# Attention and conv-gated feed-forward: from a hand-written opening and half-tile steps to periods of a whole tile

## The chip, the cores and the metric
One NeuronCore of a Trainium2 chip. TensorE (PE) multiplies matrices, with weight loads of its own (PEld); VectorE (DVE), ScalarE (ACT) and GpSimd (POOL) work elementwise; SyncE (SP) issues transfers. The metric is device microseconds of one execution. The kernel before took 697.51 us in the median of 3 runs (697.41 to 699.11).

## The reference
Eight batches of 576 tokens with 8 heads of 64: attention with a causal window of 128 tokens and a linear bias, then a feed-forward block with a gate from a convolution over three neighbouring tokens.

```python
scores = q @ k.T / 8 + slope[h] * -abs(i - j)     # where 0 <= i - j < 128, else -1e9
x = softmax(scores) @ v                           # heads side by side: (8, 576, 512)
h = maximum(x @ w_in, 0)                          # 512 -> 1024
conv = sum(conv_w[k] * h[token + k - 1] for k in range(3))
out = (h * sigmoid(conv)) @ w_out                 # 1024 -> 512
```
q, k and v are 32-bit floats; the three weight arrays are 64-bit floats, which the kernel turns into 32-bit ones on the core.

## The kernel before
The 4608 tokens are 36 tiles of 128. A tile goes through the attention in two halves (`u` = 0, 1) of four heads each:
- `load`, `loadv` (L198, L204): SP transfers q and k into `rqk`, v into `rv`.
- `qkT` (L212): PE transposes q and k (`pt`), ACT copies them to `qkT_all`.
- `scores` (L221): PE writes scores of this and the previous tile of keys to two PSUM tiles `sc` per half; DVE puts the mask in (L246) and adds the bias with a row minimum (L261), ACT exponentiates (L271), DVE divides by the sum (L279 to L281). The result is `e`.
- `attnT` (L284): PE transposes `e` (`pa`), ACT copies it to `rl` (L291), POOL cuts it into the part of this tile and of the previous one (L294, L297).
- `av` (L302), for both halves at once: PE multiplies with v, ACT and DVE split the result into a high and a low part in `x` (L323, L324). `xfin` (L335) copies one column to the neighbouring chunk (L338, L340).

The feed-forward block works on chunks of two tiles, in four steps a chunk. `up` (L349): two blocks of 12 matmuls `p` (L360), then ReLU, the convolution and the gate on ACT and DVE (`hh`, `z`), split into `gh` and `gl`. `down` (L389): 12 matmuls into `o` (L401), two steps behind `up`; after the fourth the result is copied and transferred out.

The weights come in 16 blocks of 128 x 512 and one of convolution weights. Each is transferred into `wst` (512 KB; two buffers), ACT and DVE turn its words into f32 in `wg` (`to_f32`, L122: one ACT operation, four of DVE, L129 to L136), and ACT and POOL split it into a high and a low part (L149, L150). The first two blocks go by ACT's queue into the buffer `wearly` (L163), 1 MB in all, at the very start.

All `sc`, `pt`, `pa`, `av` and `p` tiles take their PSUM banks in turn from one pool of six; `o` has two others.

The order of PE's work is the order in which the program issues it (`manual_schedule`, L487). A list of tokens, `START` (L419), writes the opening out by hand: each token is one step (`q` qkT, `c` scores, `t` attnT, `a` av, `f` a feed-forward step, `w` a weight block, `l`, `r` loads), its number a half tile (a tile, for loads). Then `STEADY` (L426) repeats once for each half tile: scores, loads, a transpose two halves ahead, attnT one half behind, av two halves behind, a feed-forward step. The other engines' orders are set by a planner from the same program and from priorities (`PRIORITY`, L427); every engine then works through its list in that order, waiting for semaphores.

Of the kernel before, what the change touches and what calls it, by code (L numbers as in the profile page):

```python
# [16 lines left out]
P = 128  # L17
# [4 lines left out]
def tile_alibi_window_attention_conv_glu(  # L22
# [31 lines left out]
    def as32(ap):  # L54
        return ap.bitcast(F32)
# [61 lines left out]
    def words(src):  # L117
        return src.bitcast(U32).rearrange("p (n t) -> p n t", t=2)
# [22 lines left out]
    def fetch_weight(src, st, eng):  # L141
        eng.dma_start(out=st, in_=words(src))
        return st

    def load_weight(dst, src, col, st=None):
        if st is None:
            st = fetch_weight(src, wpool.tile([P, WB, 2], U32, name="wst", tag="wst"), nc.sync)
        f = to_f32(st, wpool.tile([P, WB], I32, name="wg", tag="wg"))
        nc.scalar.copy(out=dst[0][:, col, :], in_=f)  # L149
        nc.gpsimd.tensor_tensor(out=dst[1][:, col, :], in0=f, in1=as32(dst[0][:, col, :]), op=ALU.subtract)  # L150

    def load_conv():
        n = 3 * NFC
        st = wpool.tile([P, WB, 2], U32, name="wst", tag="wst")[:n, :P, :]
        nc.sync.dma_start(out=st, in_=moe_conv_w.rearrange("k (f p) -> (k f) p", p=P).bitcast(U32).rearrange("r (p t) -> r p t", t=2))
        f = to_f32(st, wpool.tile([P, WB], I32, name="wg", tag="wg")[:n, :P])
        ps = pst.tile([P, n], F32, name="pcw", tag="tr")
        nc.tensor.transpose(ps, f, ident[:n, :n])
        nc.vector.tensor_copy(out=cw.rearrange("p k f -> p (k f)"), in_=ps)

    early = {}

    def fetch_early(c):  # L163
        if c == 0:
            early["t"] = xpool.tile([P, 2, WB, 2], U32, name="wearly", tag="x")
        early[c] = early["t"][:, c]
        fetch_weight(moe_w_in[c * P : (c + 1) * P, :WB], early[c], nc.scalar)

    def weight_items():
        for part in range(DFF // WB):  # L170
            for c in range(NCC):
                src = moe_w_in[c * P : (c + 1) * P, part * WB : (part + 1) * WB]
                yield lambda c=c, part=part, src=src: load_weight(
                    [w[:, :, part * WB : (part + 1) * WB] for w in wi], src, c, early[c] if part == 0 and c < 2 else None
                )
        yield load_conv
        for f in range(NFC):
            yield lambda f=f: load_weight(wo, moe_w_out[f * P : (f + 1) * P, :], f)

# [235 lines left out]

    START = """  # L419
    e0 e1 l0 r0 q1 w l1 q0 c0 w r1 q2 l2 w r2 c1 l3 t0 q3 t1 a0 c2 q4 w c3 w r3 t2 a1 q5 c4   # L420
    t3 a2 w q6 q7 c5 l4 t4 a3 w r4 c6 w w t5 a4 w l5 w w q8 r5 w c8 c7 w t6
    a5 q9 f w q10 c9 l6 a6 l7 t7 r6 w q12 w t8 f a7 q11 c10 t9 a8 f f a9 c12 
    t10 q13 q14 c11 a10 f l8 r7 r8 t11 c13 q15 t12 f a11
    """
# [4 lines left out]
    NU = 2 * NT  # L429
    NFP = NFC // 2  # L430
    downs, fns, done = [], {}, set()

    wpool = ctx.enter_context(tc.tile_pool(name="wpool", bufs=2))
    weights = list(weight_items())
    todo = [(c, i) for c in range(NCH) for i in range(NFP)]
    pos = 0

    def ffn_step(c, i):
        if c not in fns:
            fns[c] = ffn_items(c)  # L440
        fns[c][0](i)
        downs.append((c, i))
        if len(downs) > 2:
            cc, ii = downs.pop(0)
            fns[cc][1](ii)

    def step(kind, n):
        nonlocal pos
        if kind == "w":
            if weights:  # L450
                weights.pop(0)()
            return
        if kind == "f":
            if pos < len(todo):
                ffn_step(*todo[pos])
                pos += 1
            return
        if (kind, n) in done or n < 0 or n >= (NT if kind in "lr" else NU):
            return
        done.add((kind, n))  # L460
        t, u = divmod(n, 2)
        if kind == "e":
            fetch_early(n)
        elif kind == "l":
            load(n)
        elif kind == "r":
            loadv(n)
        elif kind == "q":
            qkT(t, u)
        elif kind == "c":  # L470
            scores(t, u)
        elif kind == "t":
            attnT(t, u)
        elif kind == "a":
            if u == 1:
                av(t)
                xfin(t)

    def run(kind, n=-1):
        if kind in PRIORITY:  # L480
            with tc.high_priority(PRIORITY[kind]):
                step(kind, n)
        else:
            step(kind, n)


    with tc.manual_schedule(engines={mybir.EngineType.PE}):  # L487
        for token in START.split():
            run(token[0], int(token[1:] or -1))
        n = 0  # L490
        while pos < len(todo) or n < NU + 3:
            for _ in range(3 if n else 2):
                run("w")
            t, u = divmod(n, 2)
            for token in STEADY.split():
                kind, d = token[0], int(token[1:] or 0)
                if kind in "lr":
                    if u == 1:
                        run(kind, t + d)
                elif kind == "f":  # L500
                    if n >= LAG + pos + (pos >= NFP):
                        run("f")
                else:
                    run(kind, n + d)
            n += 1
        for cc, ii in downs:
            fns[cc][1](ii)


# [26 lines left out]
```

## Time and profile before

| | us |
|---|---|
| median of 3 runs | 697.51 |
| profiled execution | 698.46 |
| its span, first to last instruction | 696.7 |
| PE busy in the span | 645.9 |
| DVE busy | 488.8 |
| ACT busy | 452.7 |
| POOL busy | 205.5 |

The span falls into an opening of about 98.6 us, in which PE has gaps, a middle up to the last `av` at about 645.4 us, and a tail of feed-forward steps. Busy times are sums over an engine's instructions; PE's matmuls overlap in the pipeline, so how long a block of matmuls holds PE is read from its start to the next block's start, not from its printed length. A granted clock of 1.00 is 2.4 GHz; the other level is half of it, 1.2 GHz, and a stretch between them has had both.

### The profile page before, as it was taken

The numbers are of one execution on the slowest core, as the hardware profiler recorded it, in microseconds if no ns is written. First come the engines' busy times: TensorE is split into PE (matmuls) and PEld (weight loads), VectorE is DVE, ScalarE is ACT, GpSimd is POOL, SyncE is SP. The second block draws the span as 40 slices with busy tenths as digits, with TensorE's granted clock in tenths as the row PEclk, the third lists the DMA queues.
The fourth block names the chain that finished last, engine by engine and source line by source line (L and its number), as shares of the span: only waits on it lengthen the run. The fifth ranks groups of instructions, "written<-read, shape, count | busy, mean of one in ns | idle before, by whom it ended". The sixth has DMA issues, their size and how long they took to land.

```text
span 696.7 us, 13447 instructions
## 1 busy us (share of the span) xinstructions
PE 645.9 (93%) x4833; PEld 546.6 (78%) x4833; DVE 488.8 (70%) x1584; ACT 452.7 (65%) x1258; POOL 205.5 (29%) x233
## 2 busy tenths in 40 slices
PE   3664489999999999999999999999999999999997
PEld 2443378888888888888888888888888888888996
DVE  6888987667776777677676677667776777677442
ACT  3664576767676767676767676767676667665563
POOL 2353442322222222222222222222222222222221
PEclk9978699999999999999999999999999999999999
DMA  9454522222322222222312222222222222000000
GB/s 247 116 152 137 137 47 47 77 47 77 62 61 47 77 46 77 47 76 47 92 31 76 47 77 46 77 47 76 62 62 46 77 47 77 16 31 1 31 32 30
DMA packets 120102, 47.02 MB, mean 67 GB/s; under 512 B 113356, under 2 KB 113380, under 8 KB 120036
## 3 DMA queue, kind: packets, MB, share of 16 engines
q1 hardware_dynamic: 119748, 45.12, 25.8%
q10 hardware_dynamic: 288, 1.05, 0.4%
q8 instruction: 38, 0.62, 0.4%
q14 instruction: 28, 0.23, 0.1%
HBM read 36.72 MB, written 9.44 MB: 66 GB/s over the span
## 4 chain that ended last, share of the span: by engine, by line
PE 86%; DVE 9%; DMA 2%; ACT 2%; issue 1%; SPq 0%; ACTq 0%
PE p L360 30%; PE o L401 28%; PE sc L239 9%; PE av L315 8%; PE pt L218 5%; PE pa L288 4%; DVE wg L136 1%; DVE sc L246 1%; DVE wst L135 1%; DVE sc L261 1%; DMA wst<-in_moe_w_out_dram 1%; DMA rqk<-in_k_dram 1%; DVE e L281 1%; DVE z L373 1%; ACT e L271 1%
## 5 line engine op out<-in xcount | busy, mean ns | idle before, releaser
L360 PE MATMUL p<-x,wi 128*128 128x258 f32 x1728 | 229.5, 290 | 7.8 <-ACT wg L128 7.8
L360 PEld LDWEIGHTS p<-x,wi 128*128 128x128 f32 x1728 | 216.5, 193 | 14.2 <-ACT wg L128 8.1
L386 POOL TENSOR_TENSOR gl<-z,gh 128x512 fp32r<-128x512 f32 x72 | 92.3, 1281 | 372.9 <-ACT gh L385 368.5
L401 PE MATMUL o<-wo,gh 128*128 128x512 f32 x576 | 180.8, 395 | 0.0
L373 DVE SCALAR_TENSOR_TENSOR z<-hh,cw,z 128x256 f32<-128x256 f32 (+7 forms) x384 | 145.9, 424 | 35.2 <-ACT z L366 32.2
L401 PEld LDWEIGHTS o<-wo,gh 128*128 128x128 f32 x576 | 103.5, 188 | 19.7
L271 ACT ACTIVATE e<-sc,st 128x128 f32<-128x128 f32 x288 | 106.3, 376 | 15.9 <-DVE st L261 11.7
L401 PE MATMUL o<-wo,gl 128*128 128x512 f32 x288 | 113.9, 396 | 0.0
L261 DVE CUSTOM_DVE_ANT_0 sc<-sc,bias 128x128 f32<-128x128 f32 x288 | 81.6, 303 | 44.0 <-ACT e L271 44.0
L379 ACT ACTIVATE z<-z 128x512 f32<-128x512 f32 x72 | 45.5, 632 | 77.4 <-DVE z L373 77.2
L365 ACT ACTIVATE hh<-p 128x258 f32<-128x258 f32 x144 | 56.1, 390 | 45.0 <-PE p L360 44.6
L380 DVE SCALAR_TENSOR_TENSOR z<-z,hh 128x512 f32<-128x512 f32 x72 | 49.8, 691 | 48.0 <-ACT z L379 48.0
L239 PE MATMUL sc<-qkT_all 64*128 64x256 f32 x512 | 76.5, 420 | 6.2 <-ACT qkT_all L219 6.2
L366 ACT ACTIVATE z<-hh,cw 128x256 f32<-128x256 f32 x144 | 74.3, 516 | 5.7
L239 PEld LDWEIGHTS sc<-qkT_all 64*128 64x128 f32 x512 | 46.6, 196 | 31.2 <-issue 14.3
L315 PE MATMUL av<-rl,rv 128*64 128x128 f32 x1088 | 69.8, 282 | 0.0
L385 ACT CAST gh<-z 128x512 fp32r<-128x512 f32 x72 | 44.6, 620 | 37.5 <-DVE z L380 37.4
L315 PEld LDWEIGHTS av<-rl,rv 128*64 128x64 f32 x1088 | 60.9, 141 | 6.8 <-issue 6.6
L401 PEld LDWEIGHTS o<-wo,gl 128*128 128x128 f32 x288 | 54.1, 188 | 13.0
L288 PE MATMUL pa<-ident_r,e 128*128 128x128 f32 x288 | 45.9, 284 | 19.3 <-DVE e L281 16.5
L218 PE MATMUL pt<-ident_r,rqk 128*128 128x128 f32 x288 | 49.9, 301 | 12.4 <-DMA rqk<-in_q_dram 6.2
L246 DVE COPY_PREDICATED sc<-m_prev,sc 128x256 f32<-128x256 uint8 x128 | 49.5, 425 | 16.0 <-PE sc L239 15.7
(62 smaller groups left out, 623.2 us busy)
## 6 DMA issues: line engine op xcount, KB each, us to landing
out_dram<-ob SPq DMA_DIRECT2D x36, 256.0 KB, 2.0
rqk<-in_q_dram SPq DMA_DIRECT2D x32, 256.0 KB, 3.3
rqk<-in_k_dram SPq DMA_DIRECT2D x32, 256.0 KB, 4.0
rv<-in_v_dram SPq DMA_DIRECT2D x32, 256.0 KB, 3.8
wst<-in_moe_w_out_dram SPq DMA_DIRECT2D x8, 512.0 KB, 3.6
wst<-in_moe_w_in_dram SPq DMA_DIRECT2D x6, 512.0 KB, 5.0
wearly<-in_moe_w_in_dram ACTq DMA_DIRECT2D x2, 512.0 KB, 5.9
rqk<-in_q_dram SPq DMA_DIRECT2D x8, 128.0 KB, 3.6
```

The source lines that it names most:

```text
L218: nc.tensor.transpose(ps[:, i, g, :], rqk[:, i, h : h + 2, :].rearrange("p h d -> p (h d)"), ident)
L239: nc.tensor.matmul(pss[a][:, g], qt, qkT_all[rows, win, u, 1, g, :], start=True, stop=True)
L246: nc.vector.copy_predicated(out=s_cur, mask=mask.unsqueeze(1).to_broadcast(shp), data=data)
L261: nc.vector.tensor_tensor_reduce(out=ps[:, g, cur, :], in0=ps[:, g, cur, :], in1=bias[:, u * HU + j, :], scale=-0.125, scalar=3.0e38, op0= ...
L271: nc.scalar.activation(out=e[:, j, :], in_=ps[:, g, cur, :], func=AF.Exp, bias=st[:, 0, j : j + 1], scale=-1.0, accum_out=st[:, 1, j : j + 1],
L288: nc.tensor.transpose(ps[:, j, :], e[:, j, :], ident)
L315: nc.tensor.matmul(ps[a * D : (a + 1) * D, u * NG + g], vraw[tt][:, u * HU + j], rl[:, side, j], start=n == 0, stop=n == len(sides) - 1,)
L360: nc.tensor.matmul(ps[:, :XW], a[:, cc, f * P : (f + 1) * P], x[:, cc, :], start=n == 0, stop=n == last)
L366: nc.scalar.activation(out=z[:, ff, :], in_=hh[:, ff, 1 : 1 + CW], func=AF.Copy, scale=cw[:, 1, f : f + 1])
L373: nc.vector.scalar_tensor_tensor(out=z[:, ff, a:cut], in0=hh[:, ff, a + kk : cut + kk], scalar=cw[:, kk, f : f + 1], in1=z[:, ff, a:cut], ...
L386: nc.gpsimd.tensor_tensor(out=gl, in0=z, in1=as32(gh), op=ALU.subtract)
L401: nc.tensor.matmul(oo[m], g[:, ff, ms], w[:, f, :], start=f == 0 and n == 0, stop=f == NFC - 1 and n == 2)
```

## The change
`START`, `STEADY` and the token machinery go. One loop runs over tiles; in each period come scores of both halves, `av` of the tile before, loads, weight blocks, a feed-forward step, both transposes `qkT` of the next tile, `attnT` of the first half, weight blocks, a feed-forward step, `attnT` of the second half. A feed-forward step `up` is taken from the seventh half tile on, one per half; `down` stays two steps behind. Weight blocks are fetched apart from their conversion: three `wst` buffers instead of two, three fetched at the start on SP's queue (none on ACT's), and a table `WEIGHTS` says how many are converted in each half of the first seven tiles. The convolution weights come as the fifth block instead of the ninth.

```diff
-    early = {}
...
+    def weight_blocks():
+        for part in range(DFF // WB):
+            cols = slice(part * WB, (part + 1) * WB)
             for c in range(NCC):
...
+                yield moe_w_in[c * P : (c + 1) * P, cols], [w[:, c, cols] for w in wi]
+            if part == 0:
+                yield None
         for f in range(NFC):
...
+            yield moe_w_out[f * P : (f + 1) * P, :], [w[:, f, :] for w in wo]
...
-    STEADY = "c0 l2 q2 t-1 a-2 r2 f"
-    PRIORITY = {'f': -15, 't': 100, 'l': 15, 'c': 60}
     LAG = 7
...
-    wpool = ctx.enter_context(tc.tile_pool(name="wpool", bufs=2))
...
+    wpool = ctx.enter_context(tc.tile_pool(name="wpool", bufs=3))
+    blocks = list(weight_blocks())
+
+    WEIGHTS = [(0, 2), (1, 1), (1, 1), (1, 1), (2, 2), (2, 2), (2, 0)]
+
+    def weight(n):
+        for _ in range(n):
+            if fetched:
+                with tc.high_priority(WPRI):
+                    convert_weight()
+            if blocks:
+                fetch_weight(blocks.pop(0))
+
+    WPRI = 0
+
+    def up(slot):
         nonlocal pos
...
+        if pos < len(todo) and pos + LAG <= slot:
...
     with tc.manual_schedule(engines={mybir.EngineType.PE}):
...
+        loads(0)
+        for _ in range(3):
+            fetch_weight(blocks.pop(0))
+        loads(1)
+        loadvs(0)
+        for u in range(2):
+            qkT(0, u)
+        for t in range(NT + 2):
+            if t < NT:
+                with tc.high_priority(60):
+                    for u in range(2):
+                        scores(t, u)
+            if 0 < t <= NT:
+                av(t - 1)
+                xfin(t - 1)
+            loads(t + 2)
+            loadvs(t + 1)
+            wa, wb = WEIGHTS[t] if t < len(WEIGHTS) else (0, 0)
+            weight(wa)
+            up(2 * t)
+            down()
+            if t + 1 < NT:
+                for u in range(2):
+                    qkT(t + 1, u)
+            if t < NT:
+                with tc.high_priority(100):
+                    attnT(t, 0)
+            weight(wb)
+            up(2 * t + 1)
+            if t < NT:
+                with tc.high_priority(100):
+                    attnT(t, 1)
+            down()
+        while pos < len(todo):
+            up(len(todo) + LAG)
+            down()
+        while downs:
+            down(0)
```

PE, middle, around tile 15, before: the end of a `down`, then one half tile of scores (`sc15_1`; the name's first number is the tile, the second the half), one transpose, one `pa`, and `av` of tile 14.
```order
L401 MATMUL o5_1_3065<-wo0_113,gl5_0_2847 128x512
L239 MATMUL sc15_1_0_3080<-qkT_all_116 128x256
L239 MATMUL sc15_1_1_3081<-qkT_all_116 128x256
L239 MATMUL sc15_1_0_3080<-qkT_all_116 128x256
L239 MATMUL sc15_1_1_3081<-qkT_all_116 128x256
L218 MATMUL pt16_1_3102<-ident_r_78,rqk16_2885 128x128 x4
L288 MATMUL pa15_0_3108<-ident_r_78,e15_0_2986 128x128 x4
L315 MATMUL av14_3117<-rl14_0_2899,rv14_2485 64x128 x2
```
The other half tile reads the same with `p` in the place of `av`. PE at the same place now:
```order
L401 MATMUL o5_1_3037<-wo0_113,gl5_0_2808 128x512
L239 MATMUL sc15_0_0_3052<-qkT_all_116 128x256
L239 MATMUL sc15_0_1_3053<-qkT_all_116 128x256
L239 MATMUL sc15_0_0_3052<-qkT_all_116 128x256
L239 MATMUL sc15_0_1_3053<-qkT_all_116 128x256
L239 MATMUL sc15_1_0_3073<-qkT_all_116 128x256
L239 MATMUL sc15_1_1_3074<-qkT_all_116 128x256
L239 MATMUL sc15_1_0_3073<-qkT_all_116 128x256
L239 MATMUL sc15_1_1_3074<-qkT_all_116 128x256
L315 MATMUL av14_3092<-rl14_0_2981,rv14_2688 64x128 x2
```
The scores of both halves stand in one run, and `av` stands right behind them. Half a period later PE has now, after a `p` pair and a `down`:
```order
L401 MATMUL o5_1_3037<-wo0_113,gl5_1_2943 128x512
L218 MATMUL pt16_0_3171<-ident_r_78,rqk16_2899 128x128 x4
L218 MATMUL pt16_1_3177<-ident_r_78,rqk16_2899 128x128 x4
L288 MATMUL pa15_0_3183<-ident_r_78,e15_0_3050 128x128 x4
L360 MATMUL p6_0_3194<-x6_2457,wi0_111 128x258 x2
```
Both transposes have left the scores and stand with `pa` of the first half; `pa` of the second half stands alone between the `p` pair and the next `down`.

DVE, opening, between the softmax of tile 2 (its last instruction is the product `e2_1`) and the masks of tile 3 (`sc3_0`), before; `wst` and `wg` are weight blocks.
```order
L281 TENSOR_TENSOR e2_1_401<-e2_1_401,st2_1_402 128x512
L136 SCALAR_TENSOR_TENSOR wg_503<-wst_501,wg_503 24x128
L324 TENSOR_TENSOR x0_330<-av1_436,x0_330 128x4x128
L129 TENSOR_SCALAR wst_521<-wst_521 128x512
L340 CAST x1_455<-x0_330 128x8
L132 TENSOR_SCALAR wst_521<-wst_521 128x512
L135 TENSOR_TENSOR wst_521<-wst_521 128x512
L129 TENSOR_SCALAR wst_534<-wst_534 128x512
L246 COPY_PREDICATED sc3_0_0_472<-m_prev_86,sc3_0_0_472 128x2x128
```
And now:
```order
L281 TENSOR_TENSOR e2_1_374<-e2_1_374,st2_1_375 128x512
L136 SCALAR_TENSOR_TENSOR wg_789<-wst_581,wg_789 128x512
L136 SCALAR_TENSOR_TENSOR wg_799<-wst_714,wg_799 128x512
L129 TENSOR_SCALAR wst_724<-wst_724 128x512
L132 TENSOR_SCALAR wst_724<-wst_724 128x512
L135 TENSOR_TENSOR wst_724<-wst_724 128x512
L129 TENSOR_SCALAR wst_797<-wst_797 128x512
L246 COPY_PREDICATED sc3_0_0_476<-m_prev_86,sc3_0_0_476 128x2x128
```
Four blocks stand here instead of three; the last, `wst_797`, is the 14th in order of the 17, where before it was the tenth and eleventh that stood here.

## Rows read from the trace of the kernel before

**Rows 1.** the page's busy times: us, share of the span, instructions
```profile
PE 645.9 (93%) x4833; PEld 546.6 (78%) x4833; DVE 488.8 (70%) x1584; ACT 452.7 (65%) x1258; POOL 205.5 (29%) x233
```

**Rows 2.** by stage: stretch, length, busy of PE, PEld, DVE, ACT, POOL, clock, DMA
```profile
0.00:80.20 80.20, 36.77 (x221) 27.14 (x221) 66.96 (x204) 42.82 (x122) 30.25 (x34) 0.82 0.61 159
...
98.60:645.40 546.80, 546.57 (x4188) 463.81 (x4188) 385.34 (x1309) 372.00 (x1057) 155.67 (x183) 1.00 0.23 57
645.40:696.80 51.40, 47.64 (x309) 42.18 (x308) 19.80 (x37) 26.06 (x50) 10.33 (x8) 1.00 0.08 31
```

**Rows 3.** timeline of PE, a middle tile: start us, us, instruction, count
```profile
204.60 3.13 PE L360 MATMUL p<-x,wi 128*128 128x258 f32 x24
207.56 0.62 PE L401 MATMUL o<-wo,gh 128*128 128x512 f32 x2
...
210.45 1.14 PE L239 MATMUL sc<-qkT_all 64*128 64x256 f32 x8
211.51 0.66 PE L218 MATMUL pt<-ident_r,rqk 128*128 128x128 f32 x4
212.00 0.60 PE L288 MATMUL pa<-ident_r,e 128*128 128x128 f32 x4
212.53 1.97 PE L315 MATMUL av<-rl,rv 128*64 128x128 f32 x32
214.43 3.15 PE L360 MATMUL p<-x,wi 128*128 128x258 f32 x24
217.42 0.62 PE L401 MATMUL o<-wo,gh 128*128 128x512 f32 x2
...
221.86 0.60 PE L288 MATMUL pa<-ident_r,e 128*128 128x128 f32 x4
222.22 3.14 PE L360 MATMUL p<-x,wi 128*128 128x258 f32 x24
```

**Rows 4.** timeline of PE, tail: o with p behind it
```profile
656.04 0.63 PE L401 MATMUL o<-wo,gh 128*128 128x512 f32 x2
...
658.83 3.06 PE L360 MATMUL p<-x,wi 128*128 128x258 f32 x24
```

**Rows 5.** timeline of PE, opening; idle before it in brackets
```profile
23.58 2.08 PE L239 MATMUL sc<-qkT_all 64*128 64x256 f32 x8
...
60.30 3.79 PE L239 MATMUL sc<-qkT_all 64*128 64x256 f32 x16 [6.21 <-ACT qkT_all L219]
...
80.44 5.44 PE L360 MATMUL p<-x,wi 128*128 128x258 f32 x24 [7.75 <-ACT wg L128]
...
87.80 0.60 PE L218 MATMUL pt<-ident_r,rqk 128*128 128x128 f32 x4
88.24 0.60 PE L288 MATMUL pa<-ident_r,e 128*128 128x128 f32 x4
```

**Rows 6.** DVE by form to 98.5 us: busy us, mean ns, idle before
```profile
L135 DVE TENSOR_TENSOR wst<-wst 128x512 uint32<-128x512 uint32 x14 | 14.0, 999 | 0.2
L136 DVE SCALAR_TENSOR_TENSOR wg<-wst,wg 128x512 f32<-128x512 f32 x14 | 11.8, 840 | 0.2
L261 DVE CUSTOM_DVE_ANT_0 sc<-sc,bias 128x128 f32<-128x128 f32 x40 | 11.2, 296 | 2.7 <-ACT e L271 2.7
L281 DVE TENSOR_TENSOR e<-e,st 128x512 f32<-128x512 f32 x10 | 8.1, 813 | 0.1
L246 DVE COPY_PREDICATED sc<-m_prev,sc 128x256 f32<-128x256 uint8 x17 | 7.2, 426 | 2.6 <-PE sc L239 2.5
...
L129 DVE TENSOR_SCALAR wst<-wst 128x512 uint32<-128x512 uint32 x14 | 6.7, 476 | 1.7 <-DMA wst<-in_moe_w_out_dram 1.7
```

**Rows 7.** k's transfers: chain in order of time; the page's DMA issues
```profile
1.29 7.31 DMA rqk<-in_k_dram
...
rqk<-in_k_dram SPq DMA_DIRECT2D x32, 256.0 KB, 4.0
```

**Rows 8.** transfers of wst, from issue to landing
```profile
DMA to landing us min/median/max: 3.2/3.8/5.2
```

More of the change, by code (lines that the diff above doesn't have):

```diff
@@ L139, in to_f32 @@
         return gf
[L141 to L159, printed above, removed]
@@ L161, in tile_alibi_window_attention_conv_glu @@
-    early = {}
[L163 to L169, printed above, removed]
+    def weight_blocks():
         for part in range(DFF // WB):
+            cols = slice(part * WB, (part + 1) * WB)
             for c in range(NCC):
[L172 to L176, printed above, removed]
-        for f in range(NFC):
-            yield lambda f=f: load_weight(wo, moe_w_out[f * P : (f + 1) * P, :], f)
+                yield moe_w_in[c * P : (c + 1) * P, cols], [w[:, c, cols] for w in wi]
+            if part == 0:
+                yield None
+        for f in range(NFC):
+            yield moe_w_out[f * P : (f + 1) * P, :], [w[:, f, :] for w in wo]
@@ new lines, in tile_alibi_window_attention_conv_glu, with fetch_weight, convert_weight @@
+    fetched = []
+    def fetch_weight(block):
+        st = wpool.tile([P, WB, 2], U32, name="wst", tag="wst")
+        if block is None:
+            n = 3 * NFC
+            st = st[:n, :P, :]
+            src = moe_conv_w.rearrange("k (f p) -> (k f) p", p=P).bitcast(U32).rearrange("r (p t) -> r p t", t=2)
+        else:
+            src = words(block[0])
+        nc.sync.dma_start(out=st, in_=src)
+        fetched.append((block, st))
+    def convert_weight():
+        block, st = fetched.pop(0)
+        g = wpool.tile([P, WB], I32, name="wg", tag="wg")
+        if block is None:
+            n = 3 * NFC
+            f = to_f32(st, g[:n, :P])
+            ps = pst.tile([P, n], F32, name="pcw", tag="tr")
+            nc.tensor.transpose(ps, f, ident[:n, :n])
+            nc.vector.tensor_copy(out=cw.rearrange("p k f -> p (k f)"), in_=ps)
+            return
+        f = to_f32(st, g)
+        hi, lo = block[1]
+        nc.scalar.copy(out=hi, in_=f)
+        nc.gpsimd.tensor_tensor(out=lo, in0=f, in1=as32(hi), op=ALU.subtract)
@@ L412, in ffn_items @@
         return up, down
[L419 to L424, printed above, removed]
-    STEADY = "c0 l2 q2 t-1 a-2 r2 f"
-    PRIORITY = {'f': -15, 't': 100, 'l': 15, 'c': 60}
-    LAG = 7
-    NU = 2 * NT
-    NFP = NFC // 2
@@ L431, in tile_alibi_window_attention_conv_glu @@
-    downs, fns, done = [], {}, set()
-    wpool = ctx.enter_context(tc.tile_pool(name="wpool", bufs=2))
-    weights = list(weight_items())
+    NFP = NFC // 2
+    LAG = 7
     todo = [(c, i) for c in range(NCH) for i in range(NFP)]
+    fns, downs = {}, []
     pos = 0
[L438 to L445, printed above, removed]
@@ L447, in step @@
-    def step(kind, n):
-        nonlocal pos
[L449 to L484, printed above, removed]
-    with tc.manual_schedule(engines={mybir.EngineType.PE}):
[L488 to L507, printed above, removed]
+    wpool = ctx.enter_context(tc.tile_pool(name="wpool", bufs=3))
@@ new lines, in tile_alibi_window_attention_conv_glu @@
+    blocks = list(weight_blocks())
[9 more added lines that the diff above has]
+    def up(slot):
+        nonlocal pos
+        if pos < len(todo) and pos + LAG <= slot:
+            c, i = todo[pos]
+            pos += 1
+            if c not in fns:
+                fns[c] = ffn_items(c)
+            with tc.high_priority(-15):
+                fns[c][0](i)
+            downs.append((c, i))
@@ new lines, in down, with loads, loadvs @@
+    def down(keep=2):
+        if len(downs) > keep:
+            c, i = downs.pop(0)
+            fns[c][1](i)
+    def loads(t):
+        if t < NT:
+            with tc.high_priority(15):
+                load(t)
+    def loadvs(t):
+        if t < NT:
+            with tc.high_priority(15):
+                loadv(t)
+    with tc.manual_schedule(engines={mybir.EngineType.PE}):
+        loads(0)
[22 more added lines that the diff above has]
+                    qkT(t + 1, u)
+            if t < NT:
+                with tc.high_priority(100):
+                    attnT(t, 0)
+            weight(wb)
+            up(2 * t + 1)
+            if t < NT:
+                with tc.high_priority(100):
[6 more added lines that the diff above has]
+            down(0)
```

## The prediction

> **What bounds the kernel now.** I read the busy times first: TensorE (PE) is busy 93% of a span of 696.7 us [rows 1]. The table by stage then cuts the span in three [rows 2]. From 98.6 to 645.4 us PE is busy 546.57 of 546.80 us at full clock (granted 1.00), with DVE at 385 and ACT at 372: here the time is the sum of what stands in PE's order, and only a shorter PE order or a new PE wait can change it. Up to 80.2 us PE is busy 36.8 us and DVE 67.0 us: this is the opening, where DVE converts the weights and computes the first softmaxes, and PE waits. After 645.4 us only feed-forward steps are left. The profiled execution took 698.46 us, 1.76 more than its span and 0.95 more than the median of 697.51; I work out a difference on its rows and take it off the median.
>
> **The tail** is the same in both: the last `av` is followed by seven `up`s, the `down`s two behind them, and three `down`s at the end. Cost 0.
>
> **The middle: the order of PE in one tile.** The PE rows in the section on the change show it: before, each half tile has scores, one transpose `pt`, one `pa`; now a tile has both scores, then `av`, and both `pt` together. Instructions and operands are the same; what changes is who stands beside whom. So I price blocks from start to start of the next block, at full clock [rows 3, 4].
> Before, one tile from 204.60 to 222.22 us, 17.62 us: p 2.96 (behind pa), o 2.89, sc 1.06, pt 0.49, pa 0.53 (av follows), av 1.90, p 2.99 (behind av), o, sc and pt again, 4.44, pa 0.36 (p follows). The same block costs more beside `sc` (64 rows of the array) or `av` (64 columns): o is 2.89 in front of sc and 2.79 in front of p; pa 0.53 in front of av and 0.36 in front of p.
> Now, by the same rows:
> - both scores: eight matmuls and their exit 1.06, plus eight more. In the opening, at half clock, sixteen in a row took 3.79 where eight took 2.08 [rows 5]: 1.71 for the second eight, 0.85 at full clock. Together 1.91.
> - av 1.90; p behind av 2.99; o in front of pt: as in front of p, 2.79.
> - both pt: four with pa behind them and no scores ahead take 88.24 − 87.80 = 0.44 [rows 5] (also beside full-array blocks), so 0.88.
> - pa 0.36 in front of p; p behind pa 2.96; pa in front of o: taken as in front of p, 0.36; o in front of sc 2.89, and 0.07 more as an allowance for a start behind pa.
> Sum 17.11 us, 0.51 less per tile. The middle holds 546.8 / 17.62 = 31 tiles: −15.8 us.
> Ends of this term: if the second scores cost 1.06, both pt 0.98 and pa in front of o 0.53, the sum is 17.59 and the gain 0.9 us; without the 0.07 it is 17.04 and the gain 18 us. I take 15.8, since the rows with the same neighbours stand in the trace and only scores to av, p to pa and pa to o do not.
> The Trainium skill (TensorEngine Tiling (Array Packing), Tiling Modes) says that changing the tiling mode, not just the tile, drains TensorE; the rows above agree in sign (0.17 between pa's two prices). It also counts scores to av, from a split by rows to a split by columns, as a change of mode; if that drain came on top of the exit inside 1.06, at 0.17, the gain would be 0.34 per tile, −10.5 us, and the time 688.5, inside the forecast's own range. The sum goes without it.
>
> **New waits in the middle.** In the new order `av` of a tile follows its `pa` of the second half by only o and both scores, 2.96 + 1.91 = 4.9 us (before: p, o, sc, pt, pa, 2.96 + 2.89 + 1.06 + 0.49 + 0.53 = 7.9 us). In that time ACT copies `rl` and POOL cuts it twice; av needs this half only at its middle, 0.95 us later. The second p block of a tile takes the PSUM bank of the tile's first scores (six banks in turn: four scores, av, then p): it comes 1.91 + 1.90 + 1.5 = 5.3 us after the tile's first score, and until then DVE must have masked and reduced, and ACT exponentiated, that block: two masks of 0.43, three reductions of 0.30 [rows 6] and the exponentials between them, about 3 us, behind the 1 us that the scores take. The slack is about 1.3 us; tiles at a batch's border have two masks more in front (0.9 us), 8 of the 31. I put 1.5 us in all for these, 0 to 6.
>
> **The opening.** What it must reach is the first `up`: PE comes to it at 80.44 us [rows 5], when the column of x has been copied (DVE L338). Before, DVE had been busy 66.96 us by then and idle 13.2 [rows 2]. What DVE has done by the same instruction now, counted in its order: 15 weights and three of four operations of the 16th, instead of 14; eight half tiles of softmax less their last normalising, instead of eight and most of a ninth. A weight is two shifts of 0.476, an exclusive-or of 0.999 and a product of 0.840, 2.79, less four overlaps of some 0.08 with the next instruction (estimate): 2.5 us. A half tile is 2 × 0.426 + 4 × 0.296 + 0.813 and two small ones, about 2.6 us [rows 6]. So 1.75 × 2.5 − 1.9 − 0.8 = +1.7: DVE is busy 68.6 us.
> Its idle time: until the first scores it has no weight to convert now, since `wearly` is gone; but k of tile 0, which took 7.31 us beside that 1 MB [rows 7], should land in about 5 (estimate, between the 4.0 us that k's transfers take in the median over the span and 7.31 [rows 7]), so the scores come at about 8 us: 5.0 us idle with the few there are while the masks are made. In the softmaxes DVE waits for ACT's exponentials, 3.4 us (2.7 stand in front of L261 in rows 6, the rest I add for L279). And the transfers: three buffers, each fetched again when its conversion is done, landing after 3.2 to 5.2 us, median 3.8 [rows 8]. DVE's order puts the first operation of the next weight ahead of the next tile's masks (the DVE rows of that section show it for the 14th weight), so a late landing holds the softmax: I find about 1.3 us at the second tile and 2.4 at the fourth. Sum 12.1 idle: the first `up` at 80.7, against 80.4. From there PE needed 18.2 us before until it never waited again (98.6 us); now it issues the first p blocks, the same scores and the same second p blocks and then waits for one half tile's softmax as before, with one pt and one pa less in between: the same to 1 us. The opening comes out at 0; its ends are −6 (no late landing, ACT hidden) and +9 (each of five rounds of transfers late by the 2 us between 3.2 and 5.2).
>
> **Sum:** −15.8 + 1.5 + 0 = −14.3: the profiled time 698.46 would be 684.2, the median 683.2 us.
>
> **Rivals.**
> - Slower: the whole-tile softmax comes too late, and the second p block (or pa) waits in each tile. For it: DVE and ACT get two half tiles of scores at once and then nothing, and the slack is 1.3 us; against it: both are 70% busy in the middle [rows 2] and 1.91 + 1.90 + 2.99 + 2.79 + 0.88 = 10.5 us lie between a tile's first score and its first pa. It decides from 0.51 us per tile on; at 1 us per tile it costs 31 − 15.8, about +15: 712 us.
> - The opening is late by its whole +9, since a waiting L129 holds all of DVE behind it. For it: 1.7 us of this wait stand in rows 6 already, with fewer weights in flight; against it: three buffers instead of two. 697.5 − 15.8 + 1.5 + 9 = 692 us.
> - The neighbours that no row shows eat the gain: 0.9 instead of 15.8: 697.5 − 0.9 + 1.5 = 698 us, no change.
> That the change doesn't do what it says is excluded by the order.
>
> **How the numbers follow.** Forecast 0.62 (its own range 678 to 689), late opening 0.14, no gain from neighbours 0.10, stalls in the middle 0.14. A measurement of this kernel can tell 0.3%, 2.1 us, from no change. Faster: 0.62 + 0.13 + 0.02 = 0.77; same 0.09; slower 0.14. The range 677 to 697 leaves out the stalls and a little at the lower end.
>
> **What would show it.** Right: the middle has PE busy throughout and a tile takes about 17.1 us; scores in runs of sixteen take 1.91; o in front of pt 2.79. Wrong: PE gaps in front of p behind ACT's exponentials (the slower rival), in front of av behind POOL's rl; a tile of 17.6 us without gaps (no gain); the first `up` after 86 us with DVE waiting for `wst` (late opening). A middle that PE no longer fills would make the whole sum wrong.

## The result, and the profile after

The changed kernel takes 690.76 us in the median of 4 runs (690.37 to 691.34), the kernel before 697.73 in the same comparison: a ratio of 0.990, 95% interval 0.9887 to 0.991. It is 7.0 us faster; 14.3 were forecast. The profiled execution took 690.37 us, with a span of 688.6, 8.1 under that of before.

The busy times first, as in [rows 1]:
```profile
PE 630.3 (92%) x4833; PEld 549.3 (80%) x4833; DVE 504.9 (73%) x1584; ACT 444.8 (65%) x1258; POOL 210.2 (31%) x233
```
PE has the same 4833 instructions and is busy 15.6 us less, but the span fell by 8.1 only; DVE has the same 1584 and is busy 16.1 us more. By stage, cut at the same marks as [rows 2] (first `up`, 98.6 us, last `av`); columns as there:
```profile
0.00:80.80 80.80, 34.06 (x213) 24.92 (x214) 70.63 (x197) 43.32 (x117) 32.79 (x36) 0.69 0.64 170
...
98.60:637.00 538.40, 531.79 (x4182) 466.83 (x4182) 399.75 (x1308) 363.84 (x1057) 160.27 (x183) 1.00 0.24 58
637.00:688.60 51.60, 47.80 (x309) 42.15 (x308) 21.21 (x39) 26.59 (x51) 11.43 (x10) 1.00 0.08 31
```
Both kernels stand at 98.6 us with nearly the same work left (4182 and 309 instructions on PE here, 4188 and 309 before), and the tail is 51.6 us against 51.4. So opening and tail moved by no more than about 1 us, and the change is in the middle: 538.4 against 546.8 us, −8.4. Of that, PE's own time is 531.79 against 546.57, −14.8; its idle time is 6.6 against 0.2, +6.4. A shorter order was won as forecast, and about half of it was lost again to waits.

The shorter order, answering to [rows 3]: a middle tile without a wait (timeline of PE, start us, us, instruction, count).
```profile
194.63 0.63 PE L401 MATMUL o<-wo,gh 128*128 128x512 f32 x2
...
197.43 1.03 PE L218 MATMUL pt<-ident_r,rqk 128*128 128x128 f32 x8
198.30 0.60 PE L288 MATMUL pa<-ident_r,e 128*128 128x128 f32 x4
198.66 3.13 PE L360 MATMUL p<-x,wi 128*128 128x258 f32 x24
201.62 0.60 PE L288 MATMUL pa<-ident_r,e 128*128 128x128 f32 x4
201.98 0.71 PE L401 MATMUL o<-wo,gh 128*128 128x512 f32 x2
...
204.95 2.00 PE L239 MATMUL sc<-qkT_all 64*128 64x256 f32 x16
206.88 1.97 PE L315 MATMUL av<-rl,rv 128*64 128x128 f32 x32
208.77 3.15 PE L360 MATMUL p<-x,wi 128*128 128x258 f32 x24
211.76 0.63 PE L401 MATMUL o<-wo,gh 128*128 128x512 f32 x2
```
From start to start: o 2.80, both pt 0.87, pa 0.36, p 2.96, pa 0.36, o 2.97, both scores 1.93, av 1.89, p 2.99: 17.13 us, where 17.11 was predicted and 17.62 stood before.

The waits of PE, whole span (us in all, times, the longest):
```profile
PE p L360 <- ACT e L271: 7.6, 10, 1.5
...
PE av L315 <- POOL rl L297: 0.8, 1, 0.8
```
Of the ten, one lies in the opening, and so does the wait in front of `av` (at 64 us); the nine of the middle (6.6 us) all stand in front of the second p block of a tile, in border tiles of a batch or beside them. This idle time is counted from the printed end of the matmul before and is less than what the waits cost: from start to start, the p pairs behind `av` take 3.31 us in the mean of 29 tiles here, and 3.00 where none of them waits (experiment 2), so the nine cost about 9 us. One of them, on PE, with the idle time in brackets:
```profile
309.49 2.00 PE L239 MATMUL sc<-qkT_all 64*128 64x256 f32 x16
311.42 1.97 PE L315 MATMUL av<-rl,rv 128*64 128x128 f32 x32
313.31 1.70 PE L360 MATMUL p<-x,wi 128*128 128x258 f32 x12
315.31 1.71 PE L360 MATMUL p<-x,wi 128*128 128x258 f32 x12 [0.30 <-ACT e L271]
```
The p block is cut in two: its second half needs the PSUM bank of the tile's first scores, and the last exponential (ACT `e`) on that bank is late. Why it is late shows on DVE in the same stretch:
```profile
301.50 2.18 DVE L373 SCALAR_TENSOR_TENSOR z<-hh,cw,z 128x192 f32<-128x192 f32 x8
...
307.79 3.66 DVE L373 SCALAR_TENSOR_TENSOR z<-hh,cw,z 128x192 f32<-128x192 f32 x8 [2.65 <-ACT z L366]
312.21 0.69 DVE L380 SCALAR_TENSOR_TENSOR z<-z,hh 128x512 f32<-128x512 f32 x1 [0.76 <-ACT z L379]
312.81 0.76 DVE L246 COPY_PREDICATED sc<-m_prev,sc 128x256 f32<-128x256 uint8 x2
```
and on POOL:
```profile
306.46 1.29 POOL L386 TENSOR_TENSOR gl<-z,gh 128x512 fp32r<-128x512 f32 x1 [9.54 <-ACT gh L385]
307.70 0.64 POOL L294 TENSOR_SCALAR_AFFINE_SELECT rl<-rl 128x512 f32<-128x512 f32 x1
...
309.69 0.63 POOL L297 TENSOR_SCALAR_AFFINE_SELECT rl<-rl 128x512 f32<-128x512 f32 x1
```
The scores started at 309.49, but their first mask started at 312.81, 3.3 us later. Before, in the same tile:
```profile
308.50 1.13 PE L239 MATMUL sc<-qkT_all 64*128 64x256 f32 x8
309.67 0.76 DVE L246 COPY_PREDICATED sc<-m_prev,sc 128x256 f32<-128x256 uint8 x2 [0.30 <-PE sc L239]
```
There the mask came 1.17 us behind the scores, and so it did in nearly every tile; now it comes 1.2 to 3.3 us behind. DVE was still on the feed-forward's `z` (L373): its eight pieces took 2.18 us at 301.50, where POOL stood idle, and 3.66 us at 307.79, where POOL worked from 306.46 to 310.3: `gl`, then the selects of both halves in a row. Over the whole span, the row of L373 (busy us, mean ns of one, idle before) before:
```profile
L373 DVE SCALAR_TENSOR_TENSOR z<-hh,cw,z 128x256 f32<-128x256 f32 (+7 forms) x384 | 145.9, 424 | 35.2 <-ACT z L366 32.2
```
and after:
```profile
L373 DVE SCALAR_TENSOR_TENSOR z<-hh,cw,z 128x256 f32<-128x256 f32 (+7 forms) x384 | 182.7, 518 | 96.8 <-ACT z L366 93.3
```
The same 384 instructions: 424 ns before, 518 ns now, 37 us more. Laid beside POOL's instructions one by one, 2 of the 384 had a select beside them before, and 133 have one now; of the whole pieces (128x256) of the changed kernel, the 101 with nothing of POOL beside them took 482 ns in the mean, the 42 with selects beside them throughout 805 ns. The Trainium skill (SBUF — State Buffer, Who interferes with whom) says that a VectorE instruction with two SBUF inputs and a GpSimd instruction that reads SBUF contend; `z` reads `hh` and `z`, the selects read `rl`, and the trace agrees, with 3.66 against 2.18 us.

The opening, answering to [rows 5] (PE):
```profile
6.74 1.65 PE L237 MATMUL sc<-qkT_all 64*128 64x128 f32 x12
...
80.82 5.22 PE L360 MATMUL p<-x,wi 128*128 128x258 f32 x24 [2.04 <-DVE st L280]
```
to [rows 6] (DVE by form to 98.5 us):
```profile
L281 DVE TENSOR_TENSOR e<-e,st 128x512 f32<-128x512 f32 x10 | 10.1, 1006 | 0.1
L129 DVE TENSOR_SCALAR wst<-wst 128x512 uint32<-128x512 uint32 x16 | 9.3, 579 | 1.0 <-DMA wst<-in_moe_w_in_dram 1.0
```
and to [rows 8] (transfers of `wst`):
```profile
DMA to landing us min/median/max: 3.2/4.2/6.5
```
The first scores came at 6.74 (predicted about 8), the first `up` at 80.82 (predicted 80.7). Weights wait for transfers 1.0 us, though the transfers are somewhat longer than before. DVE is busy 70.6 us by then (predicted 68.6): `e` takes 1006 ns where it took 813, the first weight operation 579 where it took 476. Less idle time made up for it: 10.2 us, where the prediction counted 12.1.

### The profile page after: what moved, and what is told of

It reads as the page before. It is cut to its first block, busy times and chain, and to the rows that moved or that the text cites. A ratio compares the mean times of both kernels' runs of the same rounds, so it can differ in the third digit from the quotient of the medians.

```text
span 688.6 us, 13622 instructions
## 1 busy us (share of the span) xinstructions
PE 630.3 (92%) x4833; PEld 549.3 (80%) x4833; DVE 504.9 (73%) x1584; ACT 444.8 (65%) x1258; POOL 210.2 (31%) x233
## 4 chain that ended last, share of the span: by engine, by line
DVE 45%; PE 29%; ACT 20%; issue 3%; DMA 1%; POOL 1%; ACTq 0%; SPq 0%; DVEq 0%; POOLq 0%
DVE z L373 18%; PE p L360 11%; PE o L401 11%; DVE sc L246 7%; DVE sc L261 5%; ACT e L271 4%; ACT qkT_all L219 3%; DVE e L281 3%; ACT z L379 3%; DVE z L380 2%; PE sc L239 2%; PE av L315 2%; DVE x L324 2%; DVE wst L135 2%; ACT z L366 2%
## 5 line engine op out<-in xcount | busy, mean ns | idle before, releaser
L373 DVE SCALAR_TENSOR_TENSOR z<-hh,cw,z 128x256 f32<-128x256 f32 (+7 forms) x384 | 182.7, 518 | 96.8 <-ACT z L366 93.3
L401 PE MATMUL o<-wo,gh 128*128 128x512 f32 x576 | 183.5, 400 | 0.0
L271 ACT ACTIVATE e<-sc,st 128x128 f32<-128x128 f32 x288 | 104.9, 368 | 44.6 <-DVE st L261 35.7
L379 ACT ACTIVATE z<-z 128x512 f32<-128x512 f32 x72 | 45.4, 631 | 117.4 <-DVE z L373 117.2
L261 DVE CUSTOM_DVE_ANT_0 sc<-sc,bias 128x128 f32<-128x128 f32 x288 | 80.7, 302 | 12.2 <-ACT e L271 9.3
L315 PEld LDWEIGHTS av<-rl,rv 128*64 128x64 f32 x1088 | 59.3, 138 | 13.3 <-issue 10.6
L239 PE MATMUL sc<-qkT_all 64*128 64x256 f32 x512 | 68.8, 411 | 0.0
L239 PEld LDWEIGHTS sc<-qkT_all 64*128 64x128 f32 x512 | 49.9, 199 | 16.9 <-issue 10.8
L288 PEld LDWEIGHTS pa<-ident_r,e 128*128 128x128 f32 x288 | 35.0, 147 | 35.4 <-issue 7.7
L297 POOL TENSOR_SCALAR_AFFINE_SELECT rl<-rl 128x512 f32<-128x512 f32 x72 | 52.1, 724 | 35.5 <-ACT rl L291 31.3
L365 ACT ACTIVATE hh<-p 128x258 f32<-128x258 f32 x144 | 55.5, 385 | 9.0 <-PE p L360 8.5
```

Of the source, the lines that this page charges most:

```text
L239: nc.tensor.matmul(pss[a][:, g], qt, qkT_all[rows, win, u, 1, g, :], start=True, stop=True)
L261: nc.vector.tensor_tensor_reduce(out=ps[:, g, cur, :], in0=ps[:, g, cur, :], in1=bias[:, u * HU + j, :], scale=-0.125, scalar=3.0e38, op0= ...
L271: nc.scalar.activation(out=e[:, j, :], in_=ps[:, g, cur, :], func=AF.Exp, bias=st[:, 0, j : j + 1], scale=-1.0, accum_out=st[:, 1, j : j + 1],
L288: nc.tensor.transpose(ps[:, j, :], e[:, j, :], ident)
L315: nc.tensor.matmul(ps[a * D : (a + 1) * D, u * NG + g], vraw[tt][:, u * HU + j], rl[:, side, j], start=n == 0, stop=n == len(sides) - 1,)
L373: nc.vector.scalar_tensor_tensor(out=z[:, ff, a:cut], in0=hh[:, ff, a + kk : cut + kk], scalar=cw[:, kk, f : f + 1], in1=z[:, ff, a:cut], ...
```

## The experiments

All were compared with the kernel before on the same chip, which took 697.3 to 697.8 us in each comparison; ratios are to it.

**1. The down step first.** (The kernel of this run is called kernel 1 below.) This tests whether the missing microseconds are the wait for the bank.
```diff
             weight(wa)
+            down(1)
             up(2 * t)
-            down()
```


> The changed kernel with one edit: in the first half of a period the down step (o) is issued ahead of the up step (p), so that TensorE runs scores, av, o, p instead of scores, av, p, o. Theory A (the missing 8 us are waits of a tile's second p block for the PSUM bank of the tile's first scores, which the exps empty too late in border tiles): p comes one o, about 2.8 us, later, more than the longest of the nine gaps (1.79 us), so the gaps of 0.5 to 1.8 us in front of the second p block are gone, about 8 us in all; 690.8 - 8 = 683, ratio to the kernel before 0.977 to 0.982. Prices of neighbours: p then stands behind o and in front of pt, o behind av, one visit of small blocks fewer or more nowhere, so no more than 1 us from that. Rival B (the loss is not a wait for that bank but VectorE being too busy from 100 us on): the gaps move to another instruction and the time stays at 689 to 691.

Measured: 680.7 us (680.0 to 681.4), 0.9753 [0.974, 0.9766]. The middle by the windows:
```profile
98.60:628.30 529.70, 529.70 (x4186) 468.19 (x4185) 393.48 (x1309) 370.10 (x1059) 173.09 (x185) 1.00 0.24 59
```
PE is busy 529.70 of 529.70 us. DVE is as slow on `z` as in the changed kernel, nearly:
```profile
L373 DVE SCALAR_TENSOR_TENSOR z<-hh,cw,z 128x256 f32<-128x256 f32 (+7 forms) x384 | 175.5, 489 | 92.4 <-ACT z L366 89.1
```
But the bank now has 2.9 us more to come free. So theory A holds and B falls: a nearly as busy DVE costs nothing once the first block that depends on it comes one `o` later. The gain on the changed kernel is 10.1 us by the medians, 8.9 by the spans; 8 were expected, and the waits cost about 9 from start to start. This is 17.0 us faster than before: what the neighbours' prices promised (−15.8) and about 1 us more. It is the fastest kernel of this study that computes all of the reference.

**2. No selects on POOL.** This tests what makes the exponentials late.
```diff
-        if (t * P) % S:
-            nc.gpsimd.affine_select(
-                out=l, in_=r, pattern=[[0, HU], [-1, P]], compare_op=ALU.is_ge, fill=0.0, base=-1, channel_multiplier=1
-            )
-        nc.gpsimd.affine_select(
-            out=r, in_=r, pattern=[[0, HU], [1, P]], compare_op=ALU.is_ge, fill=0.0, base=0, channel_multiplier=-1
-        )
...
-                            rl[:, side, j],
+                            rl[:, 0, j],
```


> The changed kernel without GpSimd's two selects per half (L294 and L297, that cut the exponentials into a left and a right part); the product with the values reads the uncut part for both sides, so that the window of the attention is left out of the computation. All else, masks, exps and the order on TensorE too, stays. Theory A1 (the exps are late because VectorE's z, L373, stretches beside GpSimd's work: 3.66 us for eight pieces where 2.18 us stand without it): the mean of L373 falls from 518 ns to 420 to 450 ns, most of the gaps in front of the second p block go, time 683 to 686. Rival A2 (the exps are late because a border tile has two masks more and its z is cut into eight pieces, whoever runs beside): z's mean falls or not, the gaps of 0.5 to 1.8 us stay in the same tiles, 689 to 691.

Measured: 676.0 us (675.8 to 676.0), 0.9685 [0.9671, 0.9698]. There is no wait in front of a p block after 100 us. L365 here is L373:
```profile
L365 DVE SCALAR_TENSOR_TENSOR z<-hh,cw,z 128x256 f32<-128x256 f32 (+7 forms) x384 | 146.8, 420 | 112.2 <-ACT z L358 108.0
```
The `z` of the same place in the same tile, on DVE:
```profile
298.51 1.14 DVE L365 SCALAR_TENSOR_TENSOR z<-hh,cw,z 128x192 f32<-128x192 f32 x4 [2.65 <-ACT z L358]
299.85 1.14 DVE L365 SCALAR_TENSOR_TENSOR z<-hh,cw,z 128x192 f32<-128x192 f32 x4 [0.20 <-ACT z L358]
...
302.67 0.76 DVE L246 COPY_PREDICATED sc<-m_prev,sc 128x256 f32<-128x256 uint8 x2 [0.24 <-PE sc L239]
```
Its eight pieces take 2 × 1.14 = 2.28 us instead of 3.66, and DVE is ahead: it waits 0.24 us for the scores where it was late for them, and the mask comes 1.16 us behind the scores' start (301.51), as before the change. The eight pieces and all the masks are still there, so A2 falls as a sufficient cause. The time is 7 to 10 us lower than A1 expected, since the selects slow the opening too, which I had not counted: the first `up` stands at 76.1 us instead of 80.8, with DVE busy 65.9 us by then instead of 70.6.

**3. The neighbours put back.** This takes the price of neighbours apart from all else that whole-tile periods bring. It is kernel 1 with these edits:
```diff
+            apart = t >= 6
...
                         scores(t, u)
+                    if apart and t + 1 < NT:
+                        qkT(t + 1, u)
-            if 0 < t <= NT:
+            if not apart and 0 < t <= NT:
                 av(t - 1)
...
             down(1)
+            if apart and 0 < t <= NT:
+                av(t - 1)
+                xfin(t - 1)
             up(2 * t)
-            if t + 1 < NT:
+            if not apart and t + 1 < NT:
```


> The kernel with the down step first (scores, av, o, p), with one more edit from tile 6 on: each half's scores are followed by a half of the transposes pt, and av stands behind o, so that TensorE again changes between products of 64 rows or columns and full ones six times per tile instead of three times; the same instructions, and the whole-tile periods, stay. Theory N (the gain in the middle is the price of neighbours, 0.46 us per tile): the time is 0.35 to 0.5 us x 26 tiles = 9 to 13 us above the kernel with the down step first, with about 683 there: 692 to 696. Rival M (the gain comes from something else that whole-tile periods bring, as a better cover of the exps): the same time as the kernel with the down step first, within 2 us.

Measured: 696.1 us (694.9 to 697.0, 11 runs), 0.9974 [0.9965, 0.9983]: 15.4 us over kernel 1, and nearly all of the gain over before is gone, though the instructions and the periods stay. PE has one wait, of under 1 us, after 100 us. Part of a tile on PE:
```profile
205.94 1.14 PE L239 MATMUL sc<-qkT_all 64*128 64x256 f32 x8
207.01 0.66 PE L218 MATMUL pt<-ident_r,rqk 128*128 128x128 f32 x4
207.59 1.14 PE L239 MATMUL sc<-qkT_all 64*128 64x256 f32 x8
208.66 0.66 PE L218 MATMUL pt<-ident_r,rqk 128*128 128x128 f32 x4
209.07 0.71 PE L401 MATMUL o<-wo,gh 128*128 128x512 f32 x2
```
Two runs of eight scores take 1.07 each where sixteen take 1.93; pt takes 0.58 and 0.41 where both take 0.87 together. With the rest, the medians of the blocks sum to 17.64 us per tile against 17.13 in kernel 1: 0.51 in some 29 tiles, 14.8 us of the 15.4. Theory N holds, with a price a little above the range that I gave; M falls.

**4. The old opening, then whole-tile periods.** This measures the middle alone.
The edit, against the kernel before:
```diff
             run(token[0], int(token[1:] or -1))
-        n = 0
-        while pos < len(todo) or n < NU + 3:
...
+        while weights:
+            run("w")
+        run("t", 13)
...
+        for t in range(7, NT + 2):
+            run("c", 2 * t)
+            run("c", 2 * t + 1)
+            run("a", 2 * t - 1)
...
```


> The middle of the changed kernel behind the opening of the kernel before: the written-out opening list and its weight path stand as before up to tile 6, and whole-tile periods follow from tile 7 on. Theory (the opening is worth about -1 us of the -7, the middle the rest): 690 to 693, ratio 0.989 to 0.994. Rival (the new opening brought the gain, and the middle's prices and waits cancel): 696 to 698.

Measured: 687.6 us (687.2 to 687.9), 0.9852 [0.9838, 0.9865]. The rival falls. It is 3.1 us below the changed kernel, more than expected; the waits are enough to explain it:
```profile
PE p L360 <- ACT e L271: 3.1, 5, 0.9
```
These are all five behind 98 us, against nine and 6.6 us. The feed-forward steps of this kernel stand at another place against the batch borders, so fewer border tiles have their `z` beside the selects (that this is why was not tried).

**5. The old opening with the down step first.** With the waits gone, only the openings should differ. The edit, against the kernel of experiment 4:
```diff
             run("r", t + 1)
+            down(1)
             if pos + LAG <= 2 * t:
                 up()
-            down()
```


> The opening of the kernel before up to tile 6, and from tile 7 on the whole-tile periods with the down step first. With the changed kernel's own opening these periods took 680.7. Theory (the two openings cost the same within about 1.5 us, the 3.1 us by which the old opening with the up step first, 687.6, stood under the changed kernel, 690.8, are 3.8 us less waiting for the bank): 680 to 683. Rival (the new opening itself costs about 3 us): 677 to 678.

Measured: 684.4 us (683.7 to 685.4), 0.981 [0.9797, 0.9824]: 3.7 us above kernel 1, outside of what either theory gave; the rival has the wrong sign. By the spans (682.5 against 679.7) it is 2.8 us. Of it 0.8 us is a wait in the tail, where two p pairs and two `o` steps stand in a row, and PE waits for an accumulator to be copied out:
```profile
639.42 0.73 PE L401 MATMUL o<-wo,gh 128*128 128x512 f32 x2 [0.82 <-ACT ob L407]
```
At 98.6 us the two kernels are level: PE's matmuls still to come, priced by the start-to-start times above, make 577 us in both (an estimate). From there to 125 us this run still follows the old order, with a short wait in front of `pa` at 122 us that the kernel before has too, and gets through 24.5 us of that work, kernel 1 through 26.3. So up to 98.6 us the two openings cost the same, as the theory had it; what it left out is the old order of blocks from there up to tile 6, 1.8 us, and the wait in the tail.

**6. Two stretches of small blocks per tile instead of three.** This carries the price of neighbours one step further, from kernel 1.
```diff
-            down(1)
+            down()
             up(2 * t)
+            down()
...
             if t < NT:
                 with tc.high_priority(100):
-                    attnT(t, 0)
...
-            up(2 * t + 1)
-            if t < NT:
-                with tc.high_priority(100):
-                    attnT(t, 1)
-            down()
+                    for u in range(2):
+                        attnT(t, u)
+            up(2 * t + 1)
```


> The kernel with the down step first (680.7), with the transposes pa of a tile's two halves side by side: a period on TensorE is scores, av, o, p, o, pt, pa, pa, p, with two stretches of small blocks instead of three; one more up step is pending between up and down. Theory N (each change to small blocks and back costs a fixed price): the kernel with six changes per tile measured 0.51 us per tile over that with three, 0.17 us for each; one less over 30 tiles is -5 us, 675 to 677; pa of the second half starts about 11.8 us behind the scores' end, as now, so no new wait is due. Rival W (the exps or the copies of pa, now twice in a row, come late and TensorE waits in front of pa or av): no gain, 680 to 685, with gaps in front of L288 or L315.

Measured: 684.3 us (684.2 to 684.6), 0.9809 [0.9795, 0.9822]. Theory N's number missed by 7 to 9 us, but not for rival W's reason: PE waits once in the middle, under 0.5 us. Half a tile on PE:
```profile
216.02 1.04 PE L218 MATMUL pt<-ident_r,rqk 128*128 128x128 f32 x8
216.89 1.04 PE L288 MATMUL pa<-ident_r,e 128*128 128x128 f32 x8
217.68 3.13 PE L360 MATMUL p<-x,wi 128*128 128x258 f32 x24
220.75 2.00 PE L239 MATMUL sc<-qkT_all 64*128 64x256 f32 x16
```
Two pa in a row take 0.79 us, two alone 0.36 each; and p now stands in front of the scores, 3.07 us, where o took 2.97. The medians of the blocks sum to 17.14 us per tile, against 17.13. So a fixed price for each stretch of small blocks is wrong. What went from six to three between experiment 3 and kernel 1 is another count, that of changes of the array's shape, which the rows print: 64*128 for the scores, 128*64 for `av`, 128*128 for all else, `pt` and `pa` too. A tile has six such changes before and in experiment 3, 17.62 and 17.64 us, and three in kernel 1 and here, 17.13 and 17.14: some 0.17 us for each change fits all four. A `pa` between two full blocks is no change of shape, and is no dearer alone than beside another `pa`, while in experiment 3 breaking up the scores alone cost 2 × 1.07 − 1.93 = 0.2 us per tile. What is lost against kernel 1 (3.6 us by the medians, 2.8 by the spans) lies in the opening: the first `up` now stands behind the second `pa`, on which PE waits, and comes at 83.85 instead of 80.91 us:
```profile
83.11 1.09 PE L288 MATMUL pa<-ident_r,e 128*128 128x128 f32 x4 [3.79 <-DVE e L281]
83.85 4.45 PE L360 MATMUL p<-x,wi 128*128 128x258 f32 x24
```

**7. Each select twice.** This doubles the suspected cost, in the changed kernel.
```diff
+            nc.gpsimd.affine_select(
+                out=l, in_=r, pattern=[[0, HU], [-1, P]], compare_op=ALU.is_ge, fill=0.0, base=-1, channel_multiplier=1
+            )
...
+        nc.gpsimd.affine_select(
+            out=r, in_=r, pattern=[[0, HU], [1, P]], compare_op=ALU.is_ge, fill=0.0, base=0, channel_multiplier=-1
+        )
```


> The changed kernel with each of GpSimd's two selects per half issued twice (the second finds nothing left to cut, so the values stay): GpSimd's busy time grows by about 90 us of 689, nothing on VectorE, ScalarE or TensorE is added. Theory C (VectorE's z stretches while GpSimd works, and so the exps come late): the mean of L373 rises above 518 ns, the gaps in front of the second p block grow by 0.5 to 1.5 us each and spread to further tiles, 15 to 25 us of them, and the opening, where VectorE is busy 70 of 80 us, lengthens by some 3 to 5 us: 698 to 713. Rival (z is long for another reason, and the cut parts are ready far ahead of the product that reads them): z and the gaps stay, 690 to 692.

Measured: 720.4 us (719.3 to 720.8), 1.0321 [1.0307, 1.0335]. L379 here is L373, and the waits are those of the whole span:
```profile
L379 DVE SCALAR_TENSOR_TENSOR z<-hh,cw,z 128x256 f32<-128x256 f32 (+7 forms) x384 | 199.3, 561 | 98.0 <-ACT z L372 94.5
```
```profile
PE av L321 <- POOL rl L303: 26.8, 25, 4.6
PE p L366 <- ACT e L271: 7.1, 8, 2.2
```
`z` stretches further, to 561 ns, with nothing added on DVE. The time is above theory C's range, and by another wait than it named: `av` now waits for the selects themselves. The wait for the bank grew in single tiles (its longest from 1.5 to 2.2 us), not in sum, probably since PE comes later to it, behind the waiting `av`. So the run confirms the stretching of `z` and says little on the size of the bank wait. It also shows how near the other wait stood: 4.9 us from `pa` to `av` leave no room for two more selects.

**8. No border masks.** This tests which tiles use up the slack.
```diff
-                if first + P > S:
-                    put(m_half, negb)
-                elif first < P:
-                    put(m_after, negb)
```


> The changed kernel without the two border masks (m_half and m_after, four per tile, in two tiles of the last part of each batch and the second of the next), so that those tiles' attention reaches over keys it should not: less work on VectorE only there. Theory K (three kinds of tiles use up the slack: tiles with four masks more, tiles behind a z in eight pieces, and tiles at a batch's start, whose scores take TensorE 0.84 us less and so bring the p block 0.84 us nearer): the gaps of the first kind, now 1.15, 0.51, 1.16 and 0.52 at 246, 263, 556 and 574 us, go, and the others (1.42, 1.41, 1.79 at 177, 333 and 487; 0.58 and 0.59 at 315 and 626) stay: 688 us, z's mean as before. Rival (the stretched z alone decides): all nine stay, 690 to 691.

Measured: 684.7 us (683.7 to 685.6), 0.9814 [0.9801, 0.9827]. The waits behind 98.6 us (L267 here is L271):
```profile
PE p L356 <- ACT e L267: 3.9, 5, 1.4
```
The four waits of the masked tiles are gone, and the five others stand where they were: in three tiles at a batch's start and two behind a `z` of eight pieces. Theory K holds as to which tiles. The waits fell by 2.7 us, as expected; the time is 3.3 us lower than expected, and the spans differ by 5.6, and the rest of that lies in the opening, at whose end one of these tiles stands: PE is busy 18.4 us of the 18.5 from 80 to 98.5, instead of 16.5.

## Why the prediction was right and wrong

**What failed is the term "new waits in the middle: 1.5 us in all, 0 to 6".** It measured 6.4 us of idle time more in the middle, and about 9 us from start to start: the middle of kernel 1, which has no wait, is 8.7 us shorter (529.7 against 538.4). The step had the right place (the second p block, the bank of the tile's first scores), the right tiles (border tiles) and a right slack on paper: 5.3 us against 1 + 3. What it left out is that DVE must be free when the scores come. I let the masks start about 1 us behind the scores' start; in the trace they started 3.3 us behind it, because a `z` that should end sooner took 1.5 us longer beside POOL. Experiment 2 shows it by taking POOL's selects away; experiment 7, which doubles them, shows the stretching from the other side. Experiment 1 shows that these waits are enough for what the forecast lacked: without them the time is 680.7 us, below the 683.2 that were forecast. I took DVE's durations from before, where POOL's selects stood beside 2 of 384 pieces of `z` (424 ns), and did not ask what the new order puts side by side on engines off PE's path.

**Two tile kinds were missing in that step.** The two masks more that I named explain four of nine waits, which went with 2.7 us when the masks were taken out. Three stand at a batch's start, where the scores take 1.09 us instead of 1.93 and bring p 0.84 us nearer to the bank; two stand behind a `z` in eight pieces.

**The middle's order was right in mechanism and nearly in size:** 17.11 forecast against 17.13 us per tile. For the middle −15.8 was forecast; PE's busy time says −14.8, but it holds a little of each wait, and kernel 1, without waits, says −17.1 (529.7 against 546.8), of which about 1 us is work that the opening had already done. So the waits were missed by more than the sum was, and the order gave back a part. Of the prices taken without a row, scores to av and pa to o hit to 0.02 us; the half clock that the first was scaled from was granted (0.50 from 60.30 to 64.10 us), while the 0.07 in the second was an allowance, and that it fitted is luck. Experiment 3 confirms that it is the neighbours: with the same instructions in the same periods, but the scores broken up and `av` back between full blocks, 15.4 us come back. As for the drain that the Trainium skill (TensorEngine Tiling (Array Packing), Tiling Modes) names for a change of mode: the trace agrees, with 17.64 us for six changes of shape in a tile (experiment 3) against 17.13 and 17.14 for three (kernel 1 and experiment 6). A second price between scores and av, on top of the exit, did not show (1.93 per sixteen, 1.90 per av).

**The opening was right, in part by luck:** 0 forecast, about −1 us by the trace, and level with the old one in experiment 5. Its working was less right than its sum: DVE had 2.0 us more to do than I counted and 1.9 us less idle time (of the 3.7 us of late landings that I counted, 1.0 came), and the two cancelled.

**The rivals.** The slower one (whole-tile softmax late) is what happened in part: its mechanism decides in 9 tiles, not in 31. The late opening and the neighbours that give nothing didn't come.

## What to carry to other kernels

When work is moved together, list not only what PE waits for but which instructions of the other engines now run at the same time, and give those the duration that they have beside each other; a mean from a kernel in which they stood apart is too low. A block that reuses a buffer should stand behind another block that doesn't need it: here the exchange of two neighbours in PE's order bought back 9 to 10 us with no instruction more or less. Prices of neighbours read from start to start carried to a new order within 0.02 us for pairs like those in the trace; what to count in a new order is changes of the array's shape, not stretches of small blocks.

## What the runs showed of the hardware

- DVE's `z` (two inputs in SBUF) took 3.66 us for eight pieces beside POOL's selects and subtraction, 2.18 to 2.28 without; over a whole run, 420 ns each without selects, 518 with them, 561 with twice as many.
- In the changed kernel a whole piece of `z` (128x256) took 482 ns with nothing of POOL beside it and 805 ns with selects beside it throughout.
- The same sixteen score matmuls took 1.93 us in one run, 2 × 1.07 in two. Tiles with six changes between the array shapes 64*128, 128*64 and 128*128 took 17.62 and 17.64 us, tiles with three 17.13 and 17.14, with the same instructions.
- `pa`, of the full shape, cost 0.36 us alone between two full blocks, and 0.79 for two in a row.
